# First MLP of a fused attention and two-MLP kernel: products in blocks of 384 columns over pairs of batches, v in three loads

## The chip, the cores and the metric

The kernel runs on one core of one Trainium2 chip. The metric is device time in microseconds (us), the median over runs of the whole program. Engines are named as in the profile: PE is TensorE, PEld its weight loads, DVE is VectorE, ACT is ScalarE, SP the engine that issues the transfers.

## The reference, cut to what matters

```python
def sm_attn(qq, kk, vv):
    s = scale * np.matmul(qq, kk.transpose(0, 1, 3, 2))
    a = np.exp(s - np.max(s, axis=-1, keepdims=True))
    return np.matmul(a / (np.sum(a, axis=-1, keepdims=True) + 1e-09), vv)

p_packed = sm_attn(p, k, v)                    # 8 batches, 8 heads, 32 packed rows
out = sm_attn(q, p_packed, p_packed)           # 8 batches, 8 heads, 576 tokens, 64 wide
x = out.transpose(0, 2, 1, 3).reshape(4608, 512)
h = np.maximum(x @ w_in, 0.0)                  # first MLP, 512 -> 2048 -> 512
x = (h * h) @ w_out
h = x @ w_in2                                  # second MLP, 512 -> 2048 -> 512
return (h * (1.0 / (1.0 + np.exp(-1.702 * h)))) @ w_out2
```

## The kernel before, in words

Activations stand transposed: features on the 128 partitions, tokens along the columns. The attention of a batch is short. Its output projection is folded into the first layer: per batch, `m_step` (L641) multiplies the packed values by 512 columns of `w_in` and gives M, four tiles of 512 hidden columns per batch, so that the first layer's input is the attention weights `a` of the batch, 256 rows by 576 tokens, and its weights are M, which differs from batch to batch.

The first MLP takes the tokens in blocks of 288 columns, half a batch (`HS`). A **slot** is one block and one chunk of 128 hidden rows; there are 256 of them, listed in `runs` and `slots` (L968 to L971). Work of a slot: `mm1` (token `f`, L674) makes the 128 hidden rows in PSUM; `relu` (`fr`, L689) on ACT, `square` (`fs`, L694) on ACT or DVE; `gsplit` (`g`, L706) splits the result into a high part (ACT copy) and a low part (DVE subtraction); `mm2` (`y`, L712) adds the chunk's contribution to the four accumulators of y. After a run of chunks `y_evict` (`ye`) copies the accumulators to SBUF and `y_store` (`yd`) writes them to DRAM. Chunks 0 to 7 and 8 to 15 of batches 0 and 1 are separate runs: the second loads the partial y back (`y_back`, `yl`) and adds to it.

For precision each product is three multiplications: high by high, high by low, low by high (`prod`, L249, and the list `ops` in `mm2`). So `mm1` issues 6 multiplications of 288 columns (two row groups of the 256) and `mm2` 12. Every multiplication has its own load of 128x128 weights:

```python
for (wh, wl), (xh, xl) in zip(ws, xs):
    for w, x in ((wh, xh), (wh, xl), (wl, xh)):
        nc.tensor.matmul(ps, w, x, start=start and i == 0, stop=stop and i == n - 1,
                         skip_group_check=more)
```

Four chunks of batch 0 (`full`) are done in plain float32; the change leaves them so.

The order of all this work, with the conversion of the weights from float64 words (`ld`, `ca`, `cr`, `sh`, `ad`, `or`, `us`, `uh`, `ul`), is a table of tokens, `ORDER` (L41), that is run from left to right; each engine takes its instructions in that order. What is left of the slots at the table's end is issued by a loop at the end of the kernel. `open_b` then closes the pools of the first part and opens those of the second MLP, which runs with 512 and 384 columns (`PAIRS`) in a seven-product scheme and which the change leaves as it is, except for where some of its tiles lie.

v is loaded per batch and half of the heads by `load_v` (L430), two transfers each: 4 rows of 1 KB per partition, then 64 partitions of 1 KB. M lives in a pool of 4 tiles (`m_p`), `a` in a pool of 4 (`a_p`), y in a pool of 2 (`y_p`), the transposed exponentials in a tile of their own or one of y's.

Of the kernel before, what the change touches and what calls it, by code (L numbers as in the profile page):

```python
# [26 lines left out]
NPC = NFC // 4  # L27

# [11 lines left out]
JOINT = 2  # L40
ORDER = """  # L41
q.0.0.0 p.0 k.0.0 k.0.1 q.0.1.1 ld.0 ld.1 q.0.1.0 q.0.2.0 v.0.0 v.0.1 s1.0.0 ld.2 ld.3 red.0.0.0 q.0.2.1 s1.0.1
red.0.0.1 q.0.3.0 k.1.0 q.0.0.1 red.0.1.1 red.0.1.0 ca.0 p.1 mx.0 q.0.3.1 cr.0 sh.0 mx.0 ad.0 ex.0.0.1 ex.0.0.0 or.0
ex.0.1.1 ld.4 ex.0.1.0 cr.1 warm.23 tr.0.1 e.0 e.0 ca.1 tr.0.0 ta.0.1.1 tb.0.1 ta.0.0.1 warm.4 pv.0.1 sh.1 tb.0.0 ad.1
pv.0.0 or.1 cr.2 pb.0.1.1 ca.2 st.0.0 ld.5 pb.0.0.1 ca.3 sh.2 v.1.0 warm.3 t2.0 cr.3 ad.2 v.1.1 t2.0 sh.3 warm.3
s2.0.0 or.2 ad.3 ld.6 s2.0.1 s2.0.0 s2.0.0 s2.0.0 cr.4 k.1.1 k.1.2 ca.4 s2.0.0 k.1.3 or.3 q.1.0 s2.0.0 sh.4 warm.13
m.0.0 st.0.1 s2.0.0 ld.7 cr.5 s2.0.0 s2.0.0 ca.5 s2.0.0 mh.0.0.1 mh.0.0.0 s2.0.0 s2.0.1 warm.9 f.0 s2.0.1 ad.4 f.1
or.4 fr.0 fs.0.0 f.2 sh.5 ca.6 ld.8 ad.5 fr.1 y.0 fs.1.0 sh.6 fr.2 or.5 fs.2.0 s2.0.1 ld.9 cr.6 y.1 ws.0 s2.0.1 ws.1
ad.6 s2.0.1 or.6 f.3 s2.0.1 ws.2 ld.10 s2.0.1 y.2 s2.0.1 ca.7 s2.0.1 cr.7 sh.7 fr.3 ad.7 cr.8 s1.1.0 or.7 fs.3.0 ca.8
s2.0.1 y.3 ld.11 cr.9 sh.8 as.1 ad.8 ca.9 or.8 ca.10 lw.1.0.0 f.4 sh.9 ld.12 cr.10 sh.10 f.5 ad.9 ye.3.3.0 fr.4 ad.10  # L50
ye.3.0.0 f.6 cr.11 fs.4.1 ca.11 ye.3.1.1 or.9 ye.3.2.0 y.4 fr.6 yd.3 red.1.0.0 fr.5 red.1.0.1 fs.5.0 ld.13 or.10
cp.1.0.0 st.1.0 cp.1.0.1 sh.11 y.5 ld.14 ca.12 ad.11 cr.12 or.11 fs.6.0 ws.3 sh.12 st.1.1 m.0.1 ad.12 as.0 ld.15 or.12
f.7 as.0 mh.0.1.0 ld.16 y.6 mh.0.1.1 ml.0.1.0 fr.7 ml.0.1.1 ca.13 ws.2 fs.7.0 lw.1.0.1 cr.13 s1.1.1 as.1 ws.4 sh.13
f.8 ca.14 ws.4 p.2 cr.14 red.1.1.1 f.9 q.1.1 red.1.1.0 fr.8 q.1.2 ad.13 y.7 fs.8.0 lw.1.1.0 fr.9 mx.1 mx.1 q.1.3 g.8
or.13 ex.1.0.1 k.2.0 g.8 ex.1.0.0 ld.17 f.10 ws.3 ex.1.1.1 sh.14 ex.1.1.0 f.11 ad.14 fs.9.0 tr.1.0 ca.15 e.1 e.1 y.8
ws.1 fr.11 ta.1.0 sh.15 or.14 fr.10 g.9 tb.1.0 f.12 ld.18 ws.5 fs.10.1 g.9 ws.6 pv.1.0 ws.5 g.10 ws.6 cr.15 y.9 g.10
ca.16 v.2.0 ad.15 pb.1.0.0 fr.12 sh.16 fs.12.0 tr.1.1 ws.0 g.12 y.10 or.15 fs.11.0 ta.1.1 g.12 ld.19 g.11 tb.1.1 ca.17
pv.1.1 g.11 ws.7 sh.17 ca.18 ws.7 f.13 cr.17 v.2.1 pb.1.1.1 f.14 sh.18 cr.16 ad.17 fr.13 t2.1 y.11 or.17 fr.14 t2.1
ad.16 fs.14.0 g.14 or.16 s2.1.0 ca.19 g.14 ye.11.0.0 yl.15 ld.20 f.15 sh.19 ye.11.2.0 ld.21 ye.11.3.0 s2.1.0 ye.11.1.0
y.12 s2.1.0 fs.13.0 yd.11 fr.15 s2.1.0 ws.8 g.13 s2.1.0 m.1.0 ws.9 g.13 s2.1.0 ws.8 fs.15.0 y.13 s2.1.0 g.15 lw.1.1.1  # L60
mh.1.0.1 g.15 cr.20 s2.1.0 ml.1.0.1 y.14 ca.20 s2.1.0 s2.1.0 cr.21 mh.1.0.0 s2.1.0 y.15 ca.21 ml.1.0.0 s2.1.0 sh.21
s2.1.1 s2.1.0 ye.15.0.1 f.16 ye.15.1.1 k.2.1 ye.15.3.1 f.17 k.2.2 s2.1.1 fr.16 s2.1.1 k.2.3 fs.16.0 f.18 ye.15.2.1
# [36 lines left out]
fr.70 y.66 s2.2.1 fs.70.0 fr.71 fs.71.0 y.67 g.70 g.70 s1.3.0 m.2.2 cp.3.0.0 uh.2.5 red.3.0.0 y.68 cp.3.0.1 ul.2.5
mh.2.2.1 lw.2.3.1 red.3.0.1 mh.2.2.0 ml.2.2.1 uh.2.6 y.69 lw.3.0.0 ml.2.2.0 uh.2.7 g.71 ul.2.6 g.71 ul.2.7 f.72 f.73  # L100
# [115 lines left out]


@with_exitstack
def fused_kernel(ctx, tc, qT, kF, kT, vv, pT, w_in, w_out, w_in2, w_out2, out):

# [26 lines left out]
    def prod(ps, ws, xs, start, stop, more=False):  # L249
# [935 lines left out]
```

## Time and profile before

| what | value |
|---|---|
| median of 3 runs | 1417.08 us (1416.4 to 1417.81) |
| the profiled execution's own time | 1416.51 us |
| its span on the core | 1414.7 us |
| PE busy | 1397.8 us, 9727 multiplications |
| PEld busy | 1263.4 us, 9727 loads |
| DVE busy | 968.0 us |
| ACT busy | 822.5 us |
| granted TensorE clock | full in all 40 slices |
| transfers | 307.95 MB, mean 218 GB/s |

PE's busy time is the union of its multiplications' own times, which overlap: one multiplication of 288 columns lasts 296 ns in the records, and the next begins before it ends. How fast they follow each other is read from a stretch: its time by its count. Busy shares are means over stages; the waits and the chain say what ends a stage.

### The profile page before, as it was taken

To read this page: it belongs to the slowest core of one execution; us is meant where nothing else is said; L and a number is where in the kernel's file an instruction comes from. 1 tells how busy PE (TensorE), PEld (TensorE's weight loads), DVE (VectorE), ACT (ScalarE), POOL (GpSimd) and SP (SyncE) were. 2 spreads that over 40 slices of the span, in tenths; PEclk is the share of its full clock that TensorE was granted. 3 is DMA by queue.
4 is the path that set the end of the run, shared out by engine and by line. 5 is a ranking of instruction groups with operands and counts; after the bars stand their busy time and mean duration, and the time that the engine had idled before them with its cause. 6 is when DMAs were issued, how large, how long until landed. Compare 5 with 4: busy or idle time off the path is not lost.

```text
span 1414.7 us, 24940 instructions
## 1 busy us (share of the span) xinstructions
PE 1397.8 (99%) x9727; PEld 1263.4 (89%) x9727; DVE 968.0 (68%) x1667; ACT 822.5 (58%) x1702; POOL 0.7 (0%) x6
## 2 busy tenths in 40 slices
PE   6999999999999999999999999999999999999998
PEld 4789999989999999999988888888888889999998
DVE  6999776485756758535355868577856876777685
ACT  4988757667676676755554634454445534544452
POOL 0000000000000000000000000000000000000000
PEclk9999999999999999999999999999999999999999
DMA  9879667555654755421345675556655666687684
GB/s 329 322 237 304 222 231 241 192 200 194 207 189 163 251 179 204 167 78 62 139 163 185 232 265 192 212 197 233 249 205 202 233 236 250 254 312 276 250 301 149
DMA packets 110646, 307.95 MB, mean 218 GB/s; under 512 B 9024, under 2 KB 52160, under 8 KB 96448
## 3 DMA queue, kind: packets, MB, share of 16 engines
q1 hardware_dynamic: 110528, 306.35, 62.6%
q8 instruction: 77, 1.26, 0.4%
q14 instruction: 41, 0.34, 0.1%
HBM read 250.94 MB, written 55.38 MB: 217 GB/s over the span
## 4 chain that ended last, share of the span: by engine, by line
PE 95%; DMA 2%; ACT 1%; DVE 1%; issue 0%; SPq 0%; DVEq 0%; ACTq 0%
PE h L255 38%; PE y L724 28%; PE o L255 24%; DMA raw_wo<-in_w_out 2%; PE m L458 2%; PE s L458 1%; PE pv L541 1%; DMA raw_win<-in_w_in 1%; PE tr_a L559 0%; ACT r_wo L294 0%; DVE win L307 0%; ACT e L490 0%; ACT r_win L294 0%; ACT win L289 0%; DVE wo L349 0%
## 5 line engine op out<-in xcount | busy, mean ns | idle before, releaser
L724 PE MATMUL y<-gh,wo 128*128 128x288 f32 x2976 | 425.2, 296 | 0.2
L724 PEld LDWEIGHTS y<-gh,wo 128*128 128x128 f32 x2976 | 401.6, 188 | 22.4 <-issue 16.8
L255 PE MATMUL h<-y,wA 128*128 128x512 f32 (+1 forms) x1680 | 349.1, 367 | 0.0
L255 PE MATMUL o<-g,wB 128*128 128x512 f32 (+1 forms) x1680 | 348.7, 367 | 0.0
L255 PEld LDWEIGHTS h<-y,wA 128*128 128x128 f32 x1680 | 305.7, 188 | 40.0 <-ACT r L904 0.4
L255 PEld LDWEIGHTS o<-g,wB 128*128 128x128 f32 x1680 | 305.8, 188 | 39.2
L255 PE MATMUL h<-a,M 128*128 128x288 f32 x1488 | 222.5, 296 | 0.3 <-ACT ring L692 0.3
L255 PEld LDWEIGHTS h<-a,M 128*128 128x128 f32 x1488 | 204.7, 188 | 6.6 <-ACT ring L692 2.5
L840 ACT ACTIVATE g<-hid 128x1024 fp32r<-128x1024 f32 (+1 forms) x140 | 132.8, 971 | 131.3 <-DVE hid L835 104.8
L349 DVE TENSOR_TENSOR gh<-ring,gh 128x288 fp32r<-128x288 f32 x248 | 110.3, 454 | 142.0 <-ACT gh L347 140.3
L816 DVE TENSOR_TENSOR g<-hid,g 128x1024 fp32r<-128x1024 f32 (+1 forms) x140 | 152.5, 1113 | 42.0 <-ACT g L840 40.6
L692 ACT ACTIVATE ring<-h 128x288 f32<-128x288 f32 x256 | 104.0, 408 | 81.0 <-PE h L255 78.0
L347 ACT ACTIVATE gh<-ring 128x288 fp32r<-128x288 f32 x248 | 107.0, 441 | 56.5 <-PE y L724 47.4
L904 ACT ACTIVATE r<-h 128x512 f32<-128x512 f32 (+1 forms) x120 | 66.5, 554 | 117.3 <-PE h L255 115.0
L912 DVE TENSOR_TENSOR hid<-h,r 128x512 f32<-128x512 f32 (+1 forms) x120 | 76.0, 633 | 78.2 <-PE h L255 61.7
L922 DVE TENSOR_TENSOR hid<-hid,sg 128x512 f32<-128x512 f32 (+1 forms) x120 | 75.7, 631 | 46.7 <-ACT sg L918 46.7
L918 ACT ACTIVATE sg<-hid 128x512 f32<-128x512 f32 (+1 forms) x120 | 70.2, 585 | 30.2 <-DVE hid L912 30.0
L704 ACT ACTIVATE ring<-ring 128x288 f32<-128x288 f32 x194 | 83.0, 441 | 7.5 <-DVE gh L349 3.4
L835 DVE TENSOR_TENSOR hid<-hid 128x1024 f32<-128x1024 f32 (+1 forms) x60 | 66.1, 1111 | 0.0
L391 DVE TENSOR_TENSOR wc<-sum,wc 128x256 fp32r<-128x256 f32 x64 | 25.8, 420 | 29.2 <-ACT wc L386 29.2
L658 DVE TENSOR_TENSOR M<-m,M 128x512 fp32r<-128x512 f32 x62 | 40.3, 681 | 2.9 <-ACT M L654 2.9
L918 ACT ACTIVATE sg<-h 128x512 f32<-128x512 f32 (+1 forms) x40 | 22.2, 555 | 32.1 <-PE h L255 32.1
(117 smaller groups left out, 985.6 us busy)
## 6 DMA issues: line engine op xcount, KB each, us to landing
wB<-w_d SPq DMA_DIRECT2D x70, 1024.0 KB, 5.5
wA<-w_d SPq DMA_DIRECT2D x40, 1024.0 KB, 4.9
wA<-w_d SPq DMA_DIRECT2D x40, 768.0 KB, 6.3
win<-win_d SPq DMA_DIRECT2D x56, 512.0 KB, 5.7
w_d<-wc SPq DMA_DIRECT2D x112, 256.0 KB, 3.5
y_d<-ysb SPq DMA_DIRECT2D x21, 576.0 KB, 5.1
raw_win<-in_w_in SPq DMA_DIRECT2D x16, 512.0 KB, 6.2
v<-in_vv SPq DMA_DIRECT2D x16, 512.0 KB, 5.4
```

Of the source, the lines that this page charges most:

```text
L255: nc.tensor.matmul(ps, w, x, start=start and i == 0, stop=stop and i == n - 1, skip_group_check=more)
L347: nc.scalar.activation(hi, x, AF.Copy)
L349: nc.vector.tensor_tensor(out=lo, in0=x, in1=hi.bitcast(F32), op=ALU.subtract)
L692: nc.scalar.activation(r, ps[:, :HS], AF.Relu)
L704: nc.scalar.activation(g, r, AF.Square)
L724: nc.tensor.matmul(accs[d][:, :HS], w[:, d * P:(d + 1) * P], t[:, x_, :], start=first, stop=fc == seg[1] and d not in {o[0] for o in ops[n ...
L816: nc.vector.tensor_tensor(out=t[:, :, 1, :n], in0=src, in1=t[:, :, 0, :n].bitcast(F32), op=ALU.subtract)
L840: nc.scalar.activation(t[:, :, 0, :PAIRS[p]], gop[p, i, g, "src"], AF.Copy)
L904: nc.scalar.activation(t[:, 0, :n], bank[p, c, "1"][:, :n], AF.Copy)
L912: nc.vector.tensor_tensor(out=hid(p, c, blk), in0=bank[p, c, b][:, :n], in1=part[p, c, r][:, 0, :n], op=ALU.add)
L918: nc.scalar.activation(t, bank[p, c, "1"][:, :n] if blk == 2 else hid(p, c, blk), AF.Sigmoid, scale=GELU)
L922: nc.vector.tensor_tensor(out=hid(p, c, blk), in0=bank[p, c, "1"][:, :n] if blk == 2 else hid(p, c, blk), in1=part.pop((p, c, "sg", blk)), ...
```

## The change

- The first MLP's blocks become 384 columns (`WB`), three per pair of batches: columns 0 to 383 of the first batch; the last 192 of the first with the first 192 of the second; the last 384 of the second. This holds for chunks 8 to 15 of batches 0 and 1 and for all chunks of batches 2 to 7. Chunks 0 to 7 of batches 0 and 1 stay in blocks of 288. The slots go from 256 to 200.
- M belongs to one batch, so `mm1` of a middle block is two products of 192 columns each, side by side in one PSUM tile.
- M has a fifth tile, `m5`, cut from the pool of raw weights. `a` is one tile per batch, 2 of them. y, the transposed exponentials and the second MLP's y sums share one tile, `ybig`, with one y block of 384 columns in it at a time. relu and square share 4 ring slots, square in place.
- v comes in three transfers per batch: two of 4 KB per partition, one of 64 partitions of 2 KB with the rest of both halves.
- Two items of raw weights share one tile; `unit_sums` writes one of its sums in place.
- The table `ORDER` is another.

```diff
+WB = 2 * S // 3
 ORDER = """
-red.0.0.1 q.0.3.0 k.1.0 q.0.0.1 red.0.1.1 red.0.1.0 ca.0 p.1 mx.0 q.0.3.1 cr.0 sh.0 mx.0 ad.0 ex.0.0.1 ex.0.0.0 or.0
+red.0.0.1 q.0.3.0 k.1.0 q.0.0.1 red.0.1.1 p.1 red.0.1.0 q.0.3.1 mx.0 mx.0 ex.0.0.1 ca.0 cr.0 sh.0 ex.0.0.0 ad.0
...
-    a_p = pool("a", 4)
+    a_p = pool("a", 2)
-    y_p = pool("y", 2)
+    y_p = pool("y")
+    ybig = y_p.tile([P, 4 * S], F32, tag="y", name="ybig")
...
-        vt[b, u] = t = v_p.tile([P, 5, 256], F32, tag="v", name=f"v{b}_{u}")
-        nc.sync.dma_start(out=t[:, 0:4, :], in_=vv[b, 0:512, u * 256:(u + 1) * 256].rearrange("(c p) e -> p c e", p=P))
-        nc.sync.dma_start(out=t[0:64, 4, :], in_=vv[b, 512:576, u * 256:(u + 1) * 256])
+        vt[b, u] = t = v_p.tile([P, 4, 256], F32, tag="v", name=f"v{b}_{u}")
+        nc.sync.dma_start(out=t, in_=vv[b, u])
+        if u == 0:
+            vt[b, "t"] = t = v_p.tile([64, 2, 256], F32, tag="vt", name=f"vt{b}", bufs=1)
+            nc.sync.dma_start(out=t, in_=vl[b])
...
-        if (b, f) not in M:
+        if b >= JOINT and (4 * b - 8 + f) % 5 == 4:
+            if not m5:
+                m5.append(raw_p.tile([P, 2, 2, 512], F32R, tag="raw", name="m5"))
+            M[b, f] = m5[0]
+        elif (b, f) not in M:
...
+    def cols(b, hf):
+
+        if hf < 2:
+            return [(b, hf * HS, HS)]
+        return ([(b, 0, WB)], [(b, WB, S - WB), (b + 1, 0, S - WB)], [(b + 1, S - WB, WB)])[hf - 2]
...
-            a = A[b, hf]
-            prod(ps[:, :HS], [(m[:, g, 0, c], m[:, g, 1, c]) for g in range(2)],
-                 [(a[:, g, 0, :], a[:, g, 1, :]) for g in range(2)], True, True)
+            o = 0
+            for bb, c0, n in cols(b, hf):
+                m, a = M[bb, fc // 4], ab[bb][:, :, :, c0:c0 + n]
+                prod(ps[:, o:o + n], [(m[:, g, 0, c], m[:, g, 1, c]) for g in range(2)],
+                     [(a[:, g, 0, :], a[:, g, 1, :]) for g in range(2)], True, True)
+                o += n
...
-        r = hs[b, hf, fc] = ring_tile(0, 3, HS)
-        nc.scalar.activation(r, ps[:, :HS], AF.Relu)
+        r = hs[b, hf, fc] = ring_tile(0, 3, HS) if hf < 2 else ring_tile(0, 4, WB)
+        nc.scalar.activation(r, ps[:, :r.shape[1]], AF.Relu)
...
-        t = gh[b, hf, fc] = gh_p.tile([P, 2, HS], F32R, tag="gh", name=f"gh_{b}_{hf}_{fc}")
+        t = gh[b, hf, fc] = gh_p.tile([P, 2, HS if hf < 2 else WB], F32R, tag="gh", name=f"gh_{b}_{hf}_{fc}")
...
-            nc.tensor.matmul(accs[d][:, :HS], w[:, d * P:(d + 1) * P], t[:, x_, :],
+            nc.tensor.matmul(accs[d][:, :t.shape[2]], w[:, d * P:(d + 1) * P], t[:, x_, :],
...
-    runs = [(0, 0, 0, 3), (0, 1, 0, 7), (0, 0, 4, 7), (1, 0, 0, 7), (1, 1, 0, 7),
-            (0, 0, 8, 15), (0, 1, 8, 15), (1, 0, 8, 15), (1, 1, 8, 15)]
-    runs += [(b, hf, 0, NFC - 1) for b in range(2, B) for hf in range(2)]
+    runs = [(0, 0, 0, 3), (0, 1, 0, 7), (0, 0, 4, 7), (1, 0, 0, 7), (1, 1, 0, 7)]
+    runs += [(0, 2 + j, 8, 15) for j in range(3)]
+    runs += [(b, 2 + j, 0, NFC - 1) for b in range(2, B, 2) for j in range(3)]
...
-    at(240, open_b)
+    at(184, open_b)
```

Three places show how the change moves instructions.

The first is PE in the first MLP; `h_a_c` is the first product of block a, chunk c, `y_a_d` the accumulator d of block a. Before, a middle stretch of batch 2, its second half (block 1):

```order
L255 MATMUL h_1_14_3838<-a_1_3034,M_3_3284 128x288 x6
L255 MATMUL h_1_15_3851<-a_1_3034,M_3_3284 128x288 x6
L724 MATMUL y_1_0_0_3540<-gh_1_8_3760,wo_998 128x288 x2
L724 MATMUL y_1_1_0_3543<-gh_1_8_3760,wo_998 128x288 x2
L724 MATMUL y_1_2_0_3546<-gh_1_8_3760,wo_998 128x288 x2
L724 MATMUL y_1_3_0_3549<-gh_1_8_3760,wo_998 128x288 x2
L724 MATMUL y_1_0_0_3540<-gh_1_8_3760,wo_998 128x288
L724 MATMUL y_1_1_0_3543<-gh_1_8_3760,wo_998 128x288
L724 MATMUL y_1_2_0_3546<-gh_1_8_3760,wo_998 128x288
L724 MATMUL y_1_3_0_3549<-gh_1_8_3760,wo_998 128x288
```

After the change, where the middle block (block 3) of batches 2 and 3 begins and the block ahead of it (block 2) ends:

```order
L232 MATMUL h_3_0_3396<-a_2608,M_0_2537 128x192 x6
L232 MATMUL h_3_0_3396<-a_3364,m_3295 128x192 x6
L740 MATMUL y_2_0_0_2795<-gh_2_15_3394,wo_1623 128x384 x2
L740 MATMUL y_2_1_0_2798<-gh_2_15_3394,wo_1623 128x384 x2
L740 MATMUL y_2_2_0_2801<-gh_2_15_3394,wo_1623 128x384 x2
L740 MATMUL y_2_3_0_2804<-gh_2_15_3394,wo_1623 128x384 x2
L740 MATMUL y_2_0_0_2795<-gh_2_15_3394,wo_1623 128x384
L740 MATMUL y_2_1_0_2798<-gh_2_15_3394,wo_1623 128x384
L740 MATMUL y_2_2_0_2801<-gh_2_15_3394,wo_1623 128x384
L740 MATMUL y_2_3_0_2804<-gh_2_15_3394,wo_1623 128x384
L232 MATMUL h_3_1_3429<-a_2608,M_0_2537 128x192 x6
L232 MATMUL h_3_1_3429<-a_3364,m_3295 128x192 x6
```

One chunk's `mm1` was six multiplications of 288 columns from one `a` and one M; in a middle block it is twelve of 192, six from each of two batches' `a` and M, and the `mm2` multiplications around it are 384 wide.

The second place is PE where the second batch's next M tile is made inside that middle block; `s` is the attention's second score product, `m` the M product, whose result goes to the tile that `h_3_4` (the fifth chunk) reads.

```order
L232 MATMUL h_3_3_3467<-a_2608,M_0_2537 128x192 x6
L232 MATMUL h_3_3_3467<-a_3364,m_3295 128x192 x6
...
L450 MATMUL s_3_1_1_3515<-q_3_2959,ring 32x288
L450 MATMUL m_1_0_3526<-win_1_0_2982,ring 32x512
L450 MATMUL m_1_1_3527<-win_1_0_2982,ring 32x512
...
L740 MATMUL y_3_0_0_3485<-gh_3_1_3480,wo_473 128x384 x2
...
L740 MATMUL y_3_2_0_3491<-gh_3_2_3506,wo_473 128x384
L740 MATMUL y_3_3_0_3494<-gh_3_2_3506,wo_473 128x384
L232 MATMUL h_3_4_3593<-a_2608,M_1_2666 128x192 x6
L232 MATMUL h_3_4_3593<-a_3364,M_1_3562 128x192 x6
```

The M product stands behind the fourth chunk's `mm1`, and two `mm2` (16 rows of which the first and the last two are shown) stand between it and the fifth chunk's `mm1`.

The third is the start of ACT's queue; `e` are the exponentials of batch 0's first scores, `win` and `r_win` the conversion of the first raw weights. Before:

```order
L289 ACTIVATE win_0_0_192<-raw_win_0_144 128x512
L294 ACTIVATE r_win_0_198<-raw_win_0_144 128x512
L490 ACTIVATE e_0_0_203,st_167<-s_0_1_0_174,st_167 128x288
L490 ACTIVATE e_0_0_203,st_167<-s_0_0_0_157,st_167 128x288
L490 ACTIVATE e_0_1_207,st_167<-s_0_1_1_175,st_167 128x288
L490 ACTIVATE e_0_1_207,st_167<-s_0_0_1_158,st_167 128x288
```

After:

```order
L482 ACTIVATE e_0_0_193,st_165<-s_0_1_0_170,st_165 128x288
L277 ACTIVATE win_0_0_195<-raw_124 128x512
L282 ACTIVATE r_win_0_197<-raw_124 128x512
L482 ACTIVATE e_0_0_193,st_165<-s_0_0_0_155,st_165 128x288
L482 ACTIVATE e_0_1_202,st_165<-s_0_1_1_171,st_165 128x288
L482 ACTIVATE e_0_1_202,st_165<-s_0_0_1_156,st_165 128x288
```

The first exponential now stands ahead of the first conversion instead of behind it.

## Rows read from the trace of the kernel before

**Rows 1.** The page, part 1: busy time, share of the span, instructions.

```profile
PE 1397.8 (99%) x9727; PEld 1263.4 (89%) x9727; DVE 968.0 (68%) x1667; ACT 822.5 (58%) x1702; POOL 0.7 (0%) x6
```

**Rows 2.** The page, part 4: the chain that ended last, by engine.

```profile
PE 95%; DMA 2%; ACT 1%; DVE 1%; issue 0%; SPq 0%; DVEq 0%; ACTq 0%
```

**Rows 3.** Waits of PE: line, waited for: us in total, times, longest.

```profile
PE s L458 <- DMA k<-in_kF: 6.1, 2, 5.7
PE h L680 <- ACT M L654: 1.8, 1, 1.8
PE tr_a L504 <- ACT e L490: 1.7, 2, 1.5
PE s L458 <- ACT ring L578: 1.3, 1, 1.3
PE pv L541 <- DMA v<-in_vv: 0.9, 1, 0.9
PE y L724 <- ACT win L289: 0.8, 1, 0.8
```

**Rows 4.** Groups by shape, PE: count, busy us, mean ns, idle before.

```profile
L724 PE MATMUL y<-gh,wo 128*128 128x288 f32 x2976 | 425.2, 296 | 0.2
...
L255 PEld LDWEIGHTS h<-y,wA 128*128 128x128 f32 x1680 | 305.7, 188 | 40.0 <-ACT r L904 0.4
...
L255 PE MATMUL h<-a,M 128*128 128x288 f32 x1488 | 222.5, 296 | 0.3 <-ACT ring L692 0.3
...
L458 PEld LDWEIGHTS m<-win,ring 64*32 64x32 f32 x512 | 8.9, 106 | 6.2 <-issue 1.0 <-DVE win L307 0.4 <-ACT r_wo L294 0.4
```

**Rows 5.** The chain in order of time: start us, us, what.

```profile
212.78 3.17 PE h L255 x24
...
268.12 3.17 PE y L724 x24
...
878.82 68.00 PE h L255 x300
...
1182.26 52.00 PE h L255 x300
```

**Rows 6.** Timeline of PE, 412 to 440 us: start us, us, what.

```profile
438.33 0.96 PE L255 MATMUL h<-a,M 128*128 128x288 f32 x6
```

**Rows 7.** Timeline of PE, 85.6 to 87 us, behind an M product.

```profile
85.19 1.09 PE L458 MATMUL m<-win,ring 64*32 64x512 f32 x16
86.21 1.06 PE L255 MATMUL h<-a,M 128*128 128x288 f32 x6
```

**Rows 8.** Groups by shape, ACT and DVE.

```profile
L658 DVE TENSOR_TENSOR M<-m,M 128x512 fp32r<-128x512 f32 x62 | 40.3, 681 | 2.9 <-ACT M L654 2.9
...
L654 ACT ACTIVATE M<-m 128x512 fp32r<-128x512 f32 x62 | 34.3, 597 | 3.6 <-PE m L458 3.3
L912 DVE TENSOR_TENSOR hid<-h,r 128x384 f32<-128x384 f32 x48 | 26.6, 554 | 25.8 <-PE h L255 18.5 <-ACT r L904 6.5
...
L918 ACT ACTIVATE sg<-hid 128x384 f32<-128x384 f32 x48 | 25.0, 522 | 11.1 <-DVE hid L912 10.9
...
L904 ACT ACTIVATE r<-h 128x384 f32<-128x384 f32 x48 | 23.6, 491 | 38.7 <-PE h L255 36.3
```

**Rows 9.** DMA issues: out<-in engine op xcount, KB each, median us to landing.

```profile
y_d<-ysb SPq DMA_DIRECT2D x21, 576.0 KB, 5.1
```

**Rows 10.** Timeline of ACT, 9 to 30 us; in brackets idle time before.

```profile
10.32 0.67 ACT L289 ACTIVATE win<-raw_win 128x512 f32<-128x512 f32 x1 [8.10 <-DMA raw_win<-in_w_in]
...
11.63 0.50 ACT L490 ACTIVATE e<-s,st 128x288 f32<-128x288 f32 x1
...
26.48 0.68 ACT L294 ACTIVATE r_wo<-raw_wo 128x512 int32<-128x512 uint32 x1 [1.30 <-DMA raw_wo<-in_w_out]
```

**Rows 11.** Timeline of DVE, 9 to 30 us.

```profile
9.50 0.16 DVE L481 TENSOR_TENSOR st<-st 128x2 f32<-128x2 f32 x1
...
11.37 0.16 DVE L483 TENSOR_SCALAR st<-st 128x2 f32<-128x2 f32 x1
```

More of the change, by code (lines that the diff above doesn't have):

```diff
@@ L46 @@
[L46 to L50, printed above, removed]
@@ L275, in fused_kernel @@
     st_p = poola("st", 4)
+    const = poola("const")
+    ident = const.tile([P, P], F32, name="ident")
+    one = const.tile([P, 1], F32, name="one")
+    ybig = y_p.tile([P, 4 * S], F32, tag="y", name="ybig")
     raws, wx = {}, {}
+    raw4 = [raw_p.tile([P, 2, 512], I64, tag="raw", name=f"raw{i}") for i in range(2)]
     def words(c):
@@ L370, in unit_sums @@
     def unit_sums(u):
[L371 removed]
+        t = xs[u, "s"] = cv_p.tile([P, 3, 256], F32, tag="s", name=f"sum{u}", bufs=1)
         xa, xb = xs[u, 0], xs[u, 1]
[L373 to L375 removed]
+        for o, i0, i1, op in ((t[:, 0, :], xa[:, 256:], xb[:, 256:], ALU.add), (xa[:, 256:], xa[:, :256], xa[:, 256:], ALU.subtract),
+                              (t[:, 1, :], t[:, 0, :], xa[:, :256], ALU.subtract), (t[:, 2, :], xb[:, :256], t[:, 1, :], ALU.subtract)):
+            nc.vector.tensor_tensor(out=o, in0=i0, in1=i1, op=op)
             yield
@@ L517, in e1t_tile @@
         if (b, r) not in e1T:
-            if r == 1 and (b == 0 or b >= JOINT):
-                t = y_p.tile([P, NDM * HS], F32, tag="y", name=f"e1t_{b}_{r}")[:, :5 * P]
+            if b >= JOINT:
+                t = ybig[:, 4 * S - 640 * (r + 1):4 * S - 640 * r]
             else:
-                t = e1t_p.tile([P, 5 * P], F32, tag="e1t", name=f"e1t_{b}_{r}")
+                t = ybig[:, 640 * r:640 * (r + 1)]
             e1T[b, r] = t.rearrange("p (c k) -> p c k", c=5)
@@ L614, in s2b, with batch_a @@
         nc.vector.transpose(out=x, in_=t.rearrange("p n i -> p (n i)"))
+    ab, m5 = {}, []
+    def batch_a(b):
+        if b not in ab:
+            ab[b] = a_p.tile([P, 2, 2, S], F32R, tag="a", name=f"a{b}")
+        return ab[b]
     def a_tile(b, hf):
-        a = A[b, hf] = a_p.tile([P, 4 * HS], F32R, tag="a", name=f"a{b}_{hf}").rearrange("p (u h n) -> p u h n", u=2, h=2)
+        a = A[b, hf] = batch_a(b)[:, :, :, hf * HS:(hf + 1) * HS]
         return a
@@ L732, in y_back @@
         y_tile_of(b, hf)
-        nc.sync.dma_start(out=ys[b, hf], in_=y_d[:, :, b * S + hf * HS:b * S + (hf + 1) * HS])
+        nc.sync.dma_start(out=ys[b, hf], in_=y_d[:, :, span(b, hf)])
     def y_evict(s, d, e):
@@ L764, in pair_tile, with quarter, first_tile @@
     def pair_tile(name):
-        return a_p.tile([P, 4 * HS], F32, tag="a", name=name)[:, :2 * NMAX].rearrange("p (h n) -> p h n", h=2)
+        return quarter(turn("pair", 4))
+    pairs2 = {}
+    def quarter(k):
+        if k // 2 not in pairs2:
+            pairs2[k // 2] = a_p.tile([P, 4 * NMAX], F32, tag="a", name=f"pairs{k // 2}")
+        return pairs2[k // 2][:, 2 * NMAX * (k % 2):2 * NMAX * (k % 2 + 1)].rearrange("p (h n) -> p h n", h=2)
+    def first_tile(name):
+        return quarter(turn("first", 2))
     def y_tile(name):
-        return y_p.tile([P, NDM * HS], F32, tag="y", name=name)[:, :2 * NMAX].rearrange("p (h n) -> p h n", h=2)
+        k = turn("y2", 2)
+        return ybig[:, 2 * NMAX * k:2 * NMAX * (k + 1)].rearrange("p (h n) -> p h n", h=2)
     def w_load(kind, p, n):
```

383 lines of the change are left out of this document (185 added, 198 removed).

## The prediction

> **What bounds the kernel now.** I read the page's busy times first: PE is busy 99% of the span and PEld 89%, DVE 68%, ACT 58% [rows 1]. Busy is not yet bound, so the chain of waits comes next: 95% of it is PE, 2% transfers, 1% each ACT and DVE [rows 2]. Then PE's own waits: six kinds, 12.6 us together, all of them at the kernel's start; the largest, 6.1 us, is for the first transfers [rows 3]. So behind the first 60 us or so PE never stands still for longer than a record shows, and only three things can move the time: how long PE's own stream is, the start, and waits that are not there yet.
>
> How long PE's stream is must not be read from busy time. A multiplication of 288 columns lasts 296 ns [rows 4], but 24 in a row take 3.17 us, in `mm1` and in `mm2` alike: one each **132.1 ns** [rows 5]. In the second MLP 300 of 384 columns take 52.00 us, **173.3 ns** each, and 300 of 512 take 68.00 us, 226.7 ns [rows 5]. From 384 to 512 that is 53.4 ns for 128 columns, 0.417 ns per column, and 13.3 ns that every multiplication costs whatever its width (288 columns by it: 133.3 ns, near the 132.1 measured). Wider blocks save 13.3 ns for each instruction that falls away.
>
> **What the change does, part by part.** 56 slots per block position (8 of the first pair, 3 times 16 of the others), three positions, take the place of 224 slots of 288 columns.
>
> *`mm2`.* 224 times 12 = 2688 multiplications at 132.1 ns, 355.0 us, become 168 times 12 = 2016 at 173.3 ns, 349.4 us: **5.6 us less**, all on PE and so on the path.
>
> *`mm1`.* 224 times 6 = 1344 at 132.1 ns, 177.5 us. Now the two outer blocks take 112 times 6 = 672 at 173.3 ns, 116.5 us, and the middle blocks 56 times 12 = 672 multiplications of 192 columns. Their price is in no row. By columns alone it is 173.3 less 192 times 0.417, 93.3 ns. But each has its own load of 128x128 weights, and a load needs time too. Two readings give it. Six multiplications of `mm1` take 0.96 us in the stream, where their first load ran beside the work ahead [rows 6]; behind an M product, where the first load does not begin until the small tiles are done, six take 1.06 us [rows 7]: a load that nothing hides puts about 0.10 to 0.11 us ahead of its multiplication. And a load of 32 columns lasts 106 ns, one of 128 columns 188 ns [rows 4]: 82 ns for 96 columns, or 109 ns for 128, with a part of some 79 ns that does not grow. In the stream a load begins when the multiplication ahead begins. With 288 columns, 132 ns, it is hidden; with 192 columns, 93 ns, it is not, and the loads set the pace. I take **108 ns**, between the two readings; 672 of them make 72.6 us, `mm1` 189.1 us, **11.6 us more**. The ends: 93.3 ns if the load hides after all (`mm1` 1.7 us more), and 132.1 ns, since a narrower multiplication has no reason to be dearer than one of 288 columns (27.7 us more).
>
> The skill speaks to this the other way. The Trainium skill, TensorE: Matmul & The Clock Gate, section on the weight-path perf modes, says that weights of 128 columns whose type is not FP32 are loaded over four buses at once, and these products are of the type fp32r. By that rule the load would hide and the middle blocks cost the 93.3 ns. The 0.10 us of the rows above speaks against it here, and the row decides.
>
> *PE in sum:* 11.6 less 5.6, **6.0 us more** (from 3.9 less to 22.1 more at the ends).
>
> *ACT and DVE.* The number of instructions falls by a quarter and each grows by a third in width; all of it lies beside PE. What counts is the chain of one slot: relu 0.49 us, square and copy about 0.52 each, subtraction 0.55 (the 384-column rows of the second MLP [rows 8]), 2.1 us, against two to three slots of PE ahead of its `mm2`, each 12 times 173.3 ns = 2.08 us and more. Cost 0. If that cover went, PE would wait for what is late next, the subtraction.
>
> *M tiles.* Five tiles, but a middle block uses both batches' M. So the second batch's next tile is free only behind the fourth chunk of the group ahead: three steps per pair, nine in all. Its chain is two copies of 0.597 us and the last subtraction of 0.681 [rows 8], 1.9 us behind the M product; the order has two `mm2` there, 4.16 us. On DVE two score transposes and a reduction are queued ahead of the subtractions, but they can start while PE still makes M. Cost 0; uncovered, about 1 us each.
>
> *One y block at a time.* Loading a partial y back (first pair only) now waits until the store ahead has landed. A store of 576 KB takes 5.1 us [rows 9]; 768 KB by the same rate 6.8. SP stands for that time, and the loads of `q` and `w_in` pieces behind it with it; their users are several slots of 3.1 us away. Cost 0, up to 1 us. I take **0.5 us** for these new waits together, with 0 and 4 as ends.
>
> *v and the start.* v's transfers are off the path but for 0.9 us, once [rows 3]. At the start the first exponential stands behind a conversion that waits for raw weights until 10.32 and begins at 11.63 [rows 10], with half of its bias step kept on DVE from 9.50 to 11.37 by the same conversion [rows 11]; in the new order both come first. That shortens the stretch to the first transposes by about 0.5 us (one exponential out of four). But what follows ends in a conversion at 26.48 that waits for `w_out` [rows 10], which no step moved here brings sooner. I take **0.5 us less**, with 2 less and 1 more as ends.
>
> **Sum.** The profiled execution's 1416.51 us, plus 6.0, plus 0.5, less 0.5: 1422.5. The median of the runs is 0.57 us above that execution, so **1423.1 us**. With the ends of waits and start, and 105 to 112 ns for the narrow multiplication, 1419.5 to 1427.
>
> **The rivals.** *The load hides* (faster). Place: the 672 narrow multiplications; price 93.3 ns, so PE 3.9 us less, 1413.2 us. It decides where the load takes less than 93 ns. For it: PEld's records overlap in the stream, so a load does not keep its port for all of its 188 ns. Against it: the 0.10 us. The skill's rule on loading weights named above would give this case. Chance 14%.
>
> *The fixed part comes on top.* If the 13.3 ns are a gap between a finished load and the next, a narrow multiplication takes 108 + 13 = 121 ns, 81.3 us in all, PE 14.7 us more: 1431.8 us. For it: the gap is the same at three widths. Against: at those widths the load was always ready, so it need not add. 12%.
>
> *Waits at the nine M steps or in `ybig`*, 1 us each on top of the forecast: 1432 us. It decides where DVE's queue ahead of the subtractions holds over 2.3 us more than its own chain. 8%.
>
> *The start pays it back.* PE's waits without the first transfers are 6.5 us [rows 3]; if the new table took them all away, 1416.6 us, no change. Against it: the wait for `w_out`. 10%.
>
> That the change doesn't do what it says is excluded by the order: middle blocks show twelve multiplications of 192 columns.
>
> **How the numbers follow.** The forecast has 56%. A measurement tells about 0.2%, 2.8 us, from no change: 1414.2 to 1419.9. Slower by more: 51 of the forecast's 56, all of the second and third rival, 20: 71%. Within: 5 of the forecast, 5 of the hidden load (1 us from the border), 7 of the start: 17%. Faster: 9 and 3: 12%. The range, 1413 to 1432, reaches from the hidden load to the added gap; about half of each lies outside, with a few of the third: 16 in 100.
>
> **What would show it.** Right: 672 multiplications of 128x192 with some 72 us of busy time between them, 12 in a row in 1.3 us; `mm2` 2016 times 384 columns at 173 ns; PE's waits still all in the first 60 us; the first M step's end within 1 us of before. Wrong: 12 narrow ones in 1.1 us (the load hides) or 1.45 us (the gap adds); waits of PE for ACT or DVE at `mm1` behind an M product; a first `mm1` several us earlier.

## The result, and the profile after

The changed kernel takes **1424.66 us** (median of 6 runs, 1423.05 to 1425.39); the kernel before took 1417.14 beside it (6 runs). The ratio is 1.0054, 95% interval 1.0043 to 1.0065: slower by 7.5 us, where 6.0 had been forecast. The profiled execution took 1424.72 us, its span is 1422.9 us, 8.2 us longer than before's 1414.7.

The page's part 1 of the changed kernel (busy us, share of the span, instructions) answers to [rows 1]:

```profile
PE 1408.1 (99%) x9059; PEld 1271.2 (89%) x9059; DVE 965.4 (68%) x1594; ACT 799.7 (56%) x1535; POOL 0.7 (0%) x6
```

668 multiplications fewer, and PE is busy 10 us longer. ACT and DVE have less to do than before, and the time is longer all the same: PE's own stream sets it. The waits of PE (line, waited for: us in total, times, longest) answer to [rows 3]:

```profile
PE s L450 <- DMA k<-in_kF: 6.2, 2, 6.0
PE s L450 <- DMA q<-in_qT: 1.3, 1, 1.3
PE h L693 <- ACT M L657: 1.2, 1, 1.2
PE s L450 <- ACT ring L570: 1.1, 1, 1.1
PE pv L533 <- DMA v<-in_vv: 1.1, 1, 1.1
PE h L232 <- DVE a L636: 0.4, 1, 0.4
```

All of the 11.3 us but the 0.4 for `a` lie in the first 30 us. Behind the start there is no wait at an M step, at a y block or at `mm2`. So the 8 us have to be in the stream itself, and the price of a multiplication is again read from the chain in order of time (start us, us, what), as in [rows 5]:

```profile
331.72 3.12 PE h L232 x18
...
342.12 4.16 PE y L740 x24
...
446.79 4.00 PE h L232 x36
...
729.09 73.75 PE h L232 x324
```

The 18 are `mm1` of three chunks of an outer block, 384 columns: 3.12 us / 18 = 173.3 ns each. The 24 are two `mm2`: 173.3 ns too. The 36 are `mm1` of three chunks of a middle block, 192 columns: 4.00 / 36 = **111.1 ns** each, where columns alone would have been 93.3. By the busy time of the groups (count | busy us, mean ns) this can't be seen:

```profile
L740 PE MATMUL y<-gh,wo 128*128 128x384 f32 x2016 | 372.0, 337 | 0.0
...
L232 PE MATMUL h<-a,M 128*128 128x384 f32 x576 | 110.4, 336 | 0.0
...
L232 PE MATMUL h<-a,M 128*128 128x192 f32 x576 | 69.8, 273 | 0.0
...
L232 PE MATMUL h<-a,m 128*128 128x192 f32 x96 | 13.2, 273 | 0.0
```

A narrow multiplication lasts 273 ns in these rows and starts 111 ns behind the one ahead; the two rows of 192 columns (the tile `m` is the fifth M) are the 672 that were forecast.

The last row of the chain above is where the second MLP's long runs begin, at 729.09 us. The same row of the kernel before:

```profile
720.75 73.74 PE h L255 x324
```

That is 8.3 us, all of what the span grew by; behind that point both kernels are the same.

The start of the profiled execution came out otherwise than forecast. Timeline of PE in the changed kernel (start us, us, what; in brackets the idle time before; `warm` are transposes whose result nobody uses):

```profile
20.04 0.72 PE L450 MATMUL s<-q,ring 64*32 64x288 f32 x16 [1.13 <-ACT ring L570]
22.09 1.63 PE L450 MATMUL s<-q,ring 64*32 64x288 f32 x16 [1.33 <-DMA q<-in_qT]
23.65 2.46 PE L1041 MATMUL warm<-ident 128*128 128x128 f32 x13
26.04 1.09 PE L450 MATMUL m<-win,ring 64*32 64x512 f32 x16
...
29.49 2.69 PE L693 MATMUL h<-wof,M 128*128 128x288 f32 x10 [1.23 <-ACT M L657]
```

and in the kernel before:

```profile
20.49 1.31 PE L458 MATMUL s<-q,ring 64*32 64x288 f32 x28 [1.31 <-ACT ring L578]
22.01 0.68 PE L458 MATMUL s<-q,ring 64*32 64x288 f32 x4 [0.21 <-DMA q<-in_qT]
22.62 1.64 PE L1013 MATMUL warm<-ident 128*128 128x128 f32 x13
24.18 1.61 PE L458 MATMUL m<-win,ring 64*32 64x512 f32 x16
...
28.73 3.18 PE L680 MATMUL h<-wof,M 128*128 128x288 f32 x12 [1.80 <-ACT M L654]
```

The scores begin 0.45 us sooner, as the new order meant them to, then their second half waits 1.33 us for q (0.21 before), and the same 13 transposes behind it take 2.46 us in place of 1.64. The table by stretches (stretch, us, PE, PEld, DVE, ACT, POOL busy (count), granted clock, DMA share, GB/s) says why the transposes are slow:

```profile
23.00:24.00 1.00, 1.00 (x12) 0.35 (x3) 1.00 (x2) 0.12 (x1) 0.00 (x0) 0.50 1.02 418
```

Behind the wait, from 22.0 to 25.4 us, the granted clock of this execution was 0.50, 1.2 in place of 2.4 GHz; in the kernel before it is 1.00 there. The first `mm1` comes 0.76 us later, but it hangs on neither: the M product ahead of it ends at 27.1 us, and M is copied on ACT behind a conversion that waits for `w_out`. Timeline of ACT in the changed kernel:

```profile
27.22 0.69 ACT L282 ACTIVATE r_wo<-raw 128x512 int32<-128x512 uint32 x1 [1.54 <-DMA raw<-in_w_out]
...
28.37 1.06 ACT L657 ACTIVATE M<-m 128x512 f32<-128x512 f32 x2
```

In the kernel before that conversion begins at 26.48 [rows 10]; in both kernels the first `mm1` begins some 2.26 us behind it. From 40 us on the two kernels are level: there the kernel before waits 0.8 us behind a conversion (last of [rows 3]), and the changed one does not. The eight chunks with unsplit weights end at 57.73 us in the changed kernel and at 57.77 before.

### The profile page after: what moved, and what is told of

Read it like the earlier page. It is cut to its first block, busy times and chain, and to the rows that moved or that the text cites. A ratio compares the mean times of both kernels' runs of the same rounds, so it can differ in the third digit from the quotient of the medians.

```text
span 1422.9 us, 23242 instructions
## 1 busy us (share of the span) xinstructions
PE 1408.1 (99%) x9059; PEld 1271.2 (89%) x9059; DVE 965.4 (68%) x1594; ACT 799.7 (56%) x1535; POOL 0.7 (0%) x6
## 4 chain that ended last, share of the span: by engine, by line
PE 96%; DMA 3%; ACT 1%; SPq 0%; issue 0%; DVE 0%; ACTq 0%
PE h L232 39%; PE y L740 28%; PE o L232 24%; PE m L450 2%; DMA raw<-in_w_in 1%; PE s L450 1%; PE pv L533 1%; PE h L693 1%; DMA raw<-in_w_out 1%; DMA p<-in_pT 0%; PE tr_a L551 0%; DMA q<-in_qT 0%; ACT x_wo L277 0%; ACT r_wo L282 0%; ACT win L277 0%; ACT ring L708 0%
## 5 line engine op out<-in xcount | busy, mean ns | idle before, releaser
L740 PE MATMUL y<-gh,wo 128*128 128x384 f32 (+1 forms) x2304 | 413.8, 332 | 0.0
L339 DVE TENSOR_TENSOR gh<-ring,gh 128x384 fp32r<-128x384 f32 (+1 forms) x192 | 103.1, 542 | 151.2 <-ACT gh L337 150.5
L232 PE MATMUL h<-a,M 128*128 128x384 f32 (+2 forms) x1296 | 202.3, 304 | 0.4 <-DVE a L636 0.4
L232 PEld LDWEIGHTS h<-a,M 128*128 128x128 f32 x1296 | 188.6, 189 | 5.6 <-ACT ring L708 1.9
L708 ACT ACTIVATE ring<-h 128x384 f32<-128x384 f32 (+1 forms) x200 | 94.5, 474 | 129.5 <-PE h L232 127.7
L932 ACT ACTIVATE pairs<-h 128x512 f32<-128x512 f32 (+1 forms) x120 | 66.5, 554 | 118.4 <-PE h L232 109.3
L940 DVE TENSOR_TENSOR hid<-h,pairs 128x512 f32<-128x512 f32 (+1 forms) x120 | 76.2, 635 | 78.1 <-PE h L232 61.5
L337 ACT ACTIVATE gh<-ring 128x384 fp32r<-128x384 f32 (+1 forms) x192 | 97.3, 512 | 31.5 <-PE y L740 22.0
L720 ACT ACTIVATE ring<-ring 128x384 f32<-128x384 f32 (+1 forms) x142 | 72.7, 514 | 3.8
L657 ACT ACTIVATE M<-m 128x512 fp32r<-128x512 f32 (+1 forms) x56 | 31.0, 594 | 11.6 <-PE m L450 10.3
```

Source lines behind the costliest of these rows:

```text
L337: nc.scalar.activation(hi, x, AF.Copy)
L339: nc.vector.tensor_tensor(out=lo, in0=x, in1=hi.bitcast(F32), op=ALU.subtract)
L708: nc.scalar.activation(r, ps[:, :r.shape[1]], AF.Relu)
L720: nc.scalar.activation(g, r, AF.Square)
L740: nc.tensor.matmul(accs[d][:, :t.shape[2]], w[:, d * P:(d + 1) * P], t[:, x_, :], start=first, stop=fc == seg[1] and d not in {o[0] for o ...
L932: nc.scalar.activation(t[:, 0, :n], bank[p, c, "1"][:, :n], AF.Copy)
```

## The experiments

The question was why a narrow multiplication takes 111 ns: because its load of weights does (my theory), or because something fixed comes on top of its columns. Two kernels tell these apart, one by narrower columns, one by narrower weights.

**Narrower columns.** In `cols`, the middle block:

```diff
-[(b, WB, S - WB), (b + 1, 0, S - WB)]
+[(b, WB, 128), (b, WB + 128, 64), (b + 1, 0, 64), (b + 1, 64, 128)]
```

> The changed kernel, but each middle block's columns are taken in four pieces (128, 64, 64, 128 columns) in place of two of 192, so 24 narrow multiplications per chunk in place of 12; the sums are the same. Theory (the load of 128x128 weights sets the pace of a multiplication that is shorter than it, about 111 ns whatever its width): 24 x 111 less 12 x 111 ns, times 56 chunks: 75 us more, about 1499 us; both widths at the same 111 ns. Rival (a narrow multiplication costs its columns, 0.417 ns each, and 31 ns more): 84 ns for 128 columns, 58 ns for 64, so 21 us more, about 1446 us.

Measured: 1554.67 us (2 runs), ratio 1.0967 (1.0947 to 1.0987), more than either. The chain, one run of two chunks:

```profile
499.87 2.63 PE h L232 x24
```

24 in 2.63 us are 109.6 ns each. The trace's single records, by the distance from end to end, give 112 ns where 64 columns follow 64 (median of 616) and 113 where 128 follow 128 (587): the width makes no difference. That is the theory's price; the rival's 58 and 84 ns are excluded. The records of the loads show the same from the other side (medians): in products of 288 columns and more a load begins 3 ns behind the start of the multiplication ahead, in those of 192, 128 and 64 columns 22, 52 and 83 ns behind it, and in these three the loads follow one another every 112 ns. The next load waits for the load ahead of it, no longer for the multiplication. What neither expected shows in the timeline of PE. Each row is half of a chunk, six multiplications of 128 and six of 64 columns:

```profile
288.69 2.30 PE L740 MATMUL y<-gh,wo 128*128 128x384 f32 x12
290.84 1.42 PE L232 MATMUL h<-a,M 128*128 128x128 f32 x12
292.09 1.53 PE L232 MATMUL h<-a,m 128*128 128x64 f32 x12
293.46 1.86 PE L232 MATMUL h<-a,M 128*128 128x128 f32 x12
295.14 2.80 PE L232 MATMUL h<-a,m 128*128 128x64 f32 x12
```

The same half chunk takes 1.53 us at first and 2.80 at the end. The table by stretches (stretch, us, PE, PEld, DVE, ACT, POOL busy (count), granted clock, DMA share, GB/s) says why:

```profile
290.80:293.40 2.60, 2.60 (x26) 2.60 (x24) 2.53 (x7) 0.88 (x3) 0.00 (x0) 1.00 0.04 14
293.40:294.40 1.00, 1.00 (x12) 1.00 (x10) 0.24 (x1) 0.71 (x2) 0.00 (x0) 0.99 1.00 338
294.40:295.40 1.00, 1.00 (x7) 1.00 (x6) 0.10 (x1) 0.83 (x2) 0.00 (x0) 0.50 1.01 373
```

The granted clock goes from 1.00 to 0.50, 2.4 to 1.2 GHz, with PE busy all the time. Over the whole run it is 0.962, so about 0.038 x 1552 = 59 us are lost to it, an estimate; with 56 x (24 x 109.6 less 12 x 111.1 ns) = 73 us for the pace that makes 132 us over the changed kernel, where 130 were measured. The clock falls twelve times before the end of this execution, each time in a row of three or four chunks of narrow products without an `mm2` between them.

**Narrower weights.** In `mm1`, for middle blocks, of the six terms of a product the first runs as it is and each other one twice:

```diff
+for _ in range(2 if i else 1):
+    nc.tensor.matmul(ps[:64] if i else ps, w[:, :64] if i else w, x, start=i == 0, stop=i == 10, skip_group_check=True)
```

> The changed kernel, but in the middle blocks each narrow product runs one multiplication with 128 weight columns and then ten with 64, in place of six with 128 (the second half of the rows of h gets the first term alone, so part of the product is left out). Theory (the load sets the pace; a load of 64 columns takes less than the 93 ns that 192 columns stream): 111 + 10 x 93.3 ns per product in place of 6 x 111, 112 products: 42 us more, about 1467 us, 93 ns each in the stream. Rival (about 111 ns for a multiplication of 192 columns whatever its weights): 11 x 111 per product, 62 us more, about 1487 us.

Measured: 1461.72 us (2 runs), ratio 1.0311 (1.0293 to 1.0330), 37 us over the changed kernel, where the theory had 42. The chain:

```profile
479.74 5.94 PE h L693 x66
```

66 multiplications are three chunks: 90.0 ns each. If the one with 128 weight columns takes its 111, the ten with 64 take (11 x 90.0 - 111) / 10 = 87.9 ns. The same 192 columns thus pass in 88 ns once the load is half as wide, and in 111 when it is not, and a load again begins 3 ns behind the multiplication ahead. **The load sets the pace**; the rival fell. The 87.9 ns are also less than the 93.3 that the theory took: beside the columns' 80.0 they leave some 8 ns, not 13.3. So the 13.3 ns are what a multiplication with 128 weight columns costs beside its columns, and not one of 64; what they consist of no run here shows.

**What the split costs.** In `cols`, a middle block of one product:

```diff
-[(b, WB, S - WB), (b + 1, 0, S - WB)]
+[(b, S - WB, WB)]
```

> The changed kernel, but a middle block takes all its 384 columns from the first batch and with that batch's M (the second batch's first 192 columns are left out, the first batch's are counted again). Theory (the split into two narrow products is what the change pays): 336 multiplications at 173.3 ns, 58.2 us, in place of 672 at 111, 74.7: 16.4 us less, about 1408.2 us, which is 9 us under the kernel before. Rival (part of what wider blocks save is lost elsewhere, to waits for ACT and DVE or the y blocks): 5 to 10 us less, 1415 to 1420.

Measured: 1407.72 us (4 runs; 1408.2 expected), ratio 0.9934 (0.9920 to 0.9947): 17 us under the changed kernel. So wide blocks do give what 13.3 ns for each saved multiplication promises, with this order and these y blocks; the second batch's product in the middle block takes it all back and 7 us more.

**Wider middle blocks.** If a load is hidden from some 235 columns on, the borders of the blocks are in the wrong place: 336, 480 and 336 columns make products of 240.

```diff
-WB = 2 * S // 3
+WBS = (336, 480, 336)
+WBO = (0, 336, 816, 2 * S)
...
-ring_tile(0, 4, WB)
+ring_tile(0, 3, WBS[1])[:, :WBS[hf - 2]]
```

> The changed kernel with blocks of 336, 480 and 336 columns in place of three of 384, so a middle block is two products of 240 columns; the tiles of relu's output and of g lie in one area of the same size, three in place of four for the middle blocks. Theory (the load's floor is 111 ns, which 240 columns, 113 ns, just cover): per pair of batches and chunk 12 x 153.3 + 12 x 113.3 = 3.20 us in place of 3.41, mm2 the same; 56 chunks: 11.9 us less, about 1412.8 us, 4 us under the kernel before; with waits for the three tiles up to 3 us of it lost. Rival (31 ns come on top of a narrow multiplication's columns): 131 ns for 240 columns, nothing gained, 1424.6 us.

At the borders between widths the tiles of g lie over one another in this kernel, so some chunks there take another chunk's g; the work on each engine is the same. Measured: 1418.45 us (11 runs), ratio to before 1.0008 (0.9999 to 1.0017), 6 us under the changed kernel: half of what was expected. The chain:

```profile
440.64 4.02 PE h L233 x36
444.66 2.61 PE y L750 x12
```

240 columns take 111.7 ns, so 48 columns more than in the changed kernel cost 0.6 ns: the floor, not the rival's 131. `mm2` of 480 columns takes 217.6 ns, 4 ns above the rule of columns: 672 x 4.3 ns = 2.9 us. PE also waits twice for ACT behind relu's tiles, 2.0 us in sum. Both are part of what is missing; the rest was not traced. The next run took 320, 512 and 320 columns, with areas that hand out free places for g and for relu's output; one split, that of the 183rd chunk (slot 182), comes one `mm2` later for want of a free place.

```diff
-WBS = (336, 480, 336)
+WBS = (320, 512, 320)
...
-o = 2 * w * turn(("gh", w, kind), 1536 // w)
+o = take(kind, 2 * w, 3072, key)
```

> The changed kernel with blocks of 320, 512 and 320 columns, so a middle block is two products of 256 columns; relu's output and g lie in areas of the same size as before, three tiles of 512 in place of four of 384. Theory (the load's floor of about 111 ns is covered from some 235 columns on, and each multiplication costs 13.3 ns besides its columns): 36 x 146.7 + 12 x 226.7 + 12 x 120 = 9.44 us per pair of batches and chunk in place of 9.65, 56 chunks: 11.9 us less than the changed kernel, about 1412.8 us, 4 us under the kernel before. Rival (what the run with 240 columns lacked of its 12 us is lost to waits for the three tiles, whatever the width): 1416 to 1419 us.

Measured: 1418.70 us (11 runs), ratio 1.0013 (1.0004 to 1.0022): as the rival had it. But the price was the theory's:

```profile
302.14 4.31 PE h L233 x36
...
345.22 1.76 PE h L233 x12
```

4.31 / 36 = 119.7 ns for 256 columns (forecast 120), 1.76 / 12 = 146.7 for 320. From the end of the second pair of batches to that of the third, and on to the fourth, this run gains 3.3 and 3.5 us on the changed kernel, 16 chunks at the forecast 0.21. What it lacks, it lacks in the first two pairs. Two waits of PE there that the changed kernel has not, and the timeline of ACT at the second of them:

```profile
PE m L451 <- DMA win<-win_d: 2.1, 1, 2.1
PE y L778 <- ACT gh_split L338: 1.4, 1, 1.4
```

```profile
258.72 0.67 ACT L283 ACTIVATE r_p<-raw 128x512 int32<-128x512 uint32 x1 [2.72 <-DMA raw<-in_w_in]
259.29 0.67 ACT L592 ACTIVATE s2t<-s2t 128x576 f32<-128x576 f32 x1
...
261.12 0.47 ACT L338 ACTIVATE gh_split<-ring 128x320 fp32r<-128x320 f32 x1
```

ACT comes to a conversion whose raw weights have not landed, stands for 2.7 us, and the split that PE wants is queued behind it. Behind the first of the two waits the granted clock of this execution was 0.50 as well, from 207.7 to 211.2 us, and three `mm2` there took 6.46 us that take 5.54 in the next run. The order was made for other widths, and PE now comes there sooner than the transfers. Two runs moved such places (in the order `lw` is the load of a win piece, `ca`, `cr` and `sh` are steps of a conversion, `fr` and `fs` a relu and a square, `y` an `mm2`). The first:

```diff
-v.3.0
...
-v.3.1
...
 lw.2.1.1
 cr.41
 lw.2.2.0
+v.3.0
+v.3.1
...
-cr.45
...
 y.69
+cr.45
```

> The kernel with blocks of 320, 512 and 320 columns, with two places of its order changed: batch 3's v is loaded behind the two win pieces that the M product at 208 us waited 2.9 us for, and the conversion of raw weights that held ACT 2.7 us at 256 us (and with it a split that PE waited 1.4 us for) stands one mm2 later. Theory (blocks of 320 and 512 save 3.4 us per pair of batches, as the later pairs of the run before show, and the rest of its loss was these two waits): 4 to 6 us less than that run, 1412.5 to 1414.5 us, under the kernel before. Rival (the transfers have no time to spare there, so the waits come back elsewhere): 1417 to 1419 us.

Measured: 1416.70 us (11 runs), ratio 1.0000 (0.9990 to 1.0009): 2 us less, half of what was expected or a little under. Both waits are gone (the first has 2.1 us in its row above, not 2.9). Others of the same kind are there, at 115 and 201 us, in one row of PE's waits, which had 0.6 us in the run before: a part came back elsewhere, as the rival had it.

```profile
PE h L233 <- ACT ring L741: 2.0, 2, 1.1
```

```diff
-ca.27
...
-cr.27
...
-sh.27
...
 fs.29.0
+ca.27
+cr.27
+sh.27
...
-cr.41
...
 fr.53
+cr.41
```

> The run before with two more conversions moved in the order: at 112 us and at 197 us ACT stood 1.8 us each for raw weights that had not landed, with the relus behind them that PE then waited for (1.1 and 0.9 us); they now stand behind those relus. Theory (the blocks of 320 and 512 columns are worth 4 us against the kernel before, and what is missing are such waits, set by an order made for other widths): 1.5 to 2 us less than the run before, about 1414.8 us, 2 us under the kernel before. Rival (the waits come back at the next conversion): 1416 to 1417 us.

Measured: **1415.19 us** (11 runs, 1414.10 to 1416.89), ratio to before 0.9988 (0.9979 to 0.9997), 1.6 us under the kernel before and about 9 under the changed one. It beats both, the kernel before by little: the interval ends 0.03% from no change, and it overlaps with that of the run before. That row is gone from PE's waits. In the third and the fourth pair of batches it gains 3.2 and 3.5 us on the changed kernel, as the run without the moves did, in the second 1.7; what holds back the rest of the 4 us is open.

**The other parts of the change.** v's three transfers alone, in the kernel before:

```diff
-nc.sync.dma_start(out=t[:, 0:4, :], in_=vv[b, 0:512, u * 256:(u + 1) * 256].rearrange("(c p) e -> p c e", p=P))
-nc.sync.dma_start(out=t[0:64, 4, :], in_=vv[b, 512:576, u * 256:(u + 1) * 256])
+nc.sync.dma_start(out=t, in_=vv[b, u])
+if u == 0:
+    vt[b, "t"] = t = v_p.tile([64, 2, 256], F32, tag="vt", name=f"vt{b}", bufs=1)
+    nc.sync.dma_start(out=t, in_=vl[b])
```

> The kernel before with v's three transfers of longer runs alone. Theory: v's transfers are off the path but for one wait under 1 us at the start, so within 1 us of the kernel before, 1416.3 to 1417.8. Rival (2 x 8 loads of short runs took DMA time that other loads waited for): 2 us less or more.

Measured: 1418.99 us (11 runs), ratio 1.0013 (1.0004 to 1.0022): 2.2 us slower, on neither side. Against the same multiplication in the kernel before, PE is 0.4 us ahead at 70 us, 2.0 behind at 87 and 2.9 behind at 128, and SP's own waits from 60 to 130 us have one that the kernel before has not:

```profile
SPq L435 <- PE pv L543: 5.0, 1, 5.0
```

The last 64 rows of v now have one tile for all batches. Batch 2's load stands in SP's queue until batch 1's products with v are done, and the raw weights' loads stand behind it. If the place in the queue is the price, and not the transfer, one step moved takes it back:

```diff
-v.2.0
...
 pv.1.1
+v.2.0
```

> The kernel before with v's three transfers, and batch 2's first v load moved behind batch 1's second product with v, so that SP doesn't stand for the one tile of v's last 64 rows. Theory (that stand of 5.0 us, with the raw weights' loads behind it, is all that v's new layout cost): the 2.8 us that the run with v alone lost between 82 and 123 us are gone, the time within 1 us of the kernel before. Rival (the transfers themselves cost it): 2 us over the kernel before, as in that run.

Measured: 1416.62 us (11 runs), ratio 0.9996 (0.9987 to 1.0004): no difference from before, and the row with 5.0 us has 0.7. The profiled execution was the slowest of the eleven (1418.47) and 1.1 us behind already at 70 us; from there to 128 us it loses 0.6 us, in place of 3.3. So the place in the queue was the price. The changed kernel's order has `v.2.0` behind `pv.1.1` already; there the row has 1.5 us, and PE has no wait for it.

The start, with the order of the kernel before up to the first `mm1`:

> The changed kernel with the order of the kernel before for all that comes ahead of the first mm1 (the first exponential behind the first conversion again). Theory (the new order of the start is worth under 1 us either way, and what follows hangs on w_out's load): the first mm1 within 1 us of the changed kernel's 29.5 us, the time within 1 us of 1424.7. Rival (the new order costs what the prediction thought it would gain, since q's half comes late for the scores): the first mm1 at about 28.7 us as before, the time 0.8 us less or better.

Measured: 1425.29 us (5 runs), ratio 1.0058 (1.0046 to 1.0071), against 1.0054: no difference that these runs can tell. Its timeline of PE:

```profile
21.85 1.14 PE L450 MATMUL s<-q,ring 64*32 64x288 f32 x16 [1.39 <-DMA q<-in_qT]
...
28.96 3.18 PE L693 MATMUL h<-wof,M 128*128 128x288 f32 x12 [2.25 <-ACT M L657]
```

The wait for q is there with the old order too, so the order did not make it; the granted clock stayed at 1.00 behind it and the 13 transposes took 1.64 us.

One execution is not enough to judge the start by. Eight traces have the new order up to the first `mm1`: those of the changed kernel and of the seven runs that keep its start. PE waits for q in three of them (1.3, 1.1 and 0.7 us) and not in the other five. What moves the first `mm1` is the conversion that waits for `w_out`. Timelines of ACT and PE in the last of the eight, the run with 1415.19 us:

```profile
25.76 0.68 ACT L283 ACTIVATE r_wo<-raw 128x512 int32<-128x512 uint32 x1 [0.96 <-DMA raw<-in_w_out]
28.02 3.18 PE L726 MATMUL h<-wof,M 128*128 128x288 f32 x12 [1.60 <-ACT M L658]
```

In all eight, and in the four traces with the old order (the kernel before, the two with v alone, this run), the first `mm1` begins 2.2 to 2.4 us behind the start of that conversion, whether PE waited for q or not. It begins between 27.6 and 29.5 us with the new order, median 28.2, the changed kernel's own being the latest; with the old order between 28.2 and 29.0, median 28.7. Why the same load lands up to 1.9 us earlier or later is open.

## Why the prediction was right

The sign, the size and the mechanism held; one term of the sum was a little small.

*`mm2`, 5.6 us less.* 2016 multiplications at the 173.3 ns that were taken for them. Right.

*`mm1`, 11.6 us more.* The outer blocks came at 173.3 ns. The narrow ones were taken at 108 ns, with 105 and 112 as bounds, and took 111.1: 672 x 3.1 ns = 2.1 us more than the term, so `mm1` grew by 13.7 us. That is the term that was too small. Its reason, that loads set the pace below the width which hides them, is shown by the two runs with narrower columns and narrower weights. The 13.3 ns "whatever its width" hold for loads of 128 weight columns, the only ones in this sum.

*PE in sum, 6.0 us more.* 13.7 less 5.6 is 8.1, and the chain shows 8.3 at the second MLP's first long run. What is left for waits, M tiles, y blocks and the start together is 0.2 us, where their terms of 0.5 more and 0.5 less made nothing.

*The start, 0.5 us less.* The last step of this term held: in all twelve traces the first `mm1` hangs on the conversion that waits for `w_out`. By that step the exponential that was moved brings nothing, so the 0.5 us had no ground; the medians, 28.2 against 28.7 us, are no proof of it, since executions with one order lie up to 1.9 us apart. The 0.76 us that the profiled execution came later had no effect on the end.

*v, off the path.* The transfers are, but the prediction looked at their waits alone and not at SP's queue behind the one tile for the last rows. In the old order that costs some 2 us, which the new order avoids; that the prediction came out right here was luck.

*ACT and DVE, M tiles and y blocks, cost 0.* Right: behind the start PE has one wait in the trace, 0.4 us for `a`.

*The ends.* Added up, the terms' ends give 1419.1 to 1430.8 us, not 1419.5 to 1427; the measured time lies in both.

*The rivals.* The hidden load (93.3 ns, 1413.2 us) is excluded by 111.1 ns at 192 columns and 109.6 at 64 and 128. By the Trainium skill, TensorE: Matmul & The Clock Gate, section on the weight-path perf modes, weights of 128 columns whose type is not FP32 are loaded over four buses at once, and by that rule the load should have hidden. The 111.1 ns speak against it for these products; they are of the type fp32r and the rows list their loads as f32, so whether the rule is meant for them stays open. The added gap (121 ns, 1431.8 us) is excluded by the same rows: the 13.3 ns do not come on top of a load. The waits at the M steps and the start that pays back did not come.

## What to carry to other kernels

A multiplication with weights of its own has a floor, here about 111 ns or 235 columns. Before a block is laid across two operands, work out the narrowest piece that this leaves: 13.3 ns are saved for each instruction that falls away, and 18 ns were lost for each one of 192 columns, where 256 columns lose nothing.

An order written out for one set of widths has to be gone through again when the widths change: a conversion that waits for a transfer takes everything behind it on its engine along. And of an added transfer, look at what is queued behind it, not only at who waits for its data.

## What was not expected of the hardware

With multiplications of 64 and 128 columns PE was busy all the time and the granted clock still fell to 0.50, each time in a row of such chunks without an `mm2` between them; the pace of the loads fell with it (half a chunk in 2.80 us in place of 1.53), so a load is paced by TensorE's clock too. With 192 columns the same succession of three chunks stayed at the full pace (36 in 4.00 us), at a granted clock of 1.00.
